# A fused attention and SwiGLU kernel on one core: other first loads, another place for two weight conversions, and DMA issue order left to the planner from the fourth pair on

## The chip, the cores and the metric

One core of one Trainium2 chip runs the whole kernel in one launch. The metric is the device time of the execution in microseconds. TensorE's granted clock is shown by the profile as a share of full speed; its two levels are 1.2 and 2.4 GHz.

## The reference

Attention over 4 batches of 8 heads, 576 positions and head size 64, with rotary embedding; its output, transposed to 2304 tokens by 512, goes through a SwiGLU block with 1536 hidden columns. All arrays are float32.

```
rotate(x) = [x1*cos - x2*sin, x1*sin + x2*cos]          # x1, x2: halves of the head
s   = rotate(q) @ rotate(k)^T / sqrt(64)
p   = exp(s - max(s)) ; p = p / (sum(p) + 1e-9)
x   = (p @ v) as 2304 x 512
out = (silu(x @ w_gate) * (x @ w_val)) @ w_out
```

## The kernel before

**Pairs and steps.** The 32 heads are worked as 16 pairs of heads. A pair has nine blocks of query rows, so there are 144 steps, n = 9p + b. Step n issues the score matmuls of block n+1 (`scores`, line 348), their row maximum on VectorE (`peak`, 363), the exponential on ScalarE (`exp`, 381), the transposes of the exponentials of block n-1 (`trans`, 424), with their high and low parts (425, 426), and some of the matmuls with V (`pv_some`, 464). All products are made from a high part and a low part of each operand.

**What a pair needs first.** `load_qk` (170) brings Q and K of a pair into one of two buffers X. `rope` (209 to 211), on GpSimd, rotates them with the tables `tab`. `qk_T` transposes the result on TensorE, and its high and low parts go to the tile N (307, 311). `qk_stack` (318 to 325) is eight DMAs of N, within SBUF, into QK, QZ and BD, from which most scores are computed; blocks 0 to 5, 9 and 10 read N directly. `load_v` (187) brings V into the one buffer VR, and `vsplit` (277, 278), on GpSimd, makes its two parts in VS.

**Start.** `start()` does the first pair by hand: VectorE rotates K (`turn(ve, 0, 1, ...)`) and the first rows of Q, GpSimd the rest. `warm` issues matmuls whose result nobody reads. ScalarE scales the table for Q (238). The table comes in three pieces on ScalarE's DMA queue, the first X in four on SyncE's.

**Two weight conversions within the attention.** `wfirst(0, i)` loads a block of the gate weights (i = 0) or value weights (i = 1) into the one buffer R (752) and returns nine operations (`bits10`: ScalarE takes the absolute value at 734, GpSimd clamps at 709, VectorE does bit work at 736 to 739, ScalarE copies at 710, GpSimd ends at 712 and 713). `PLAN["cv"]` holds for each i the step of the load and then the steps of the nine operations. Two more such conversions, `conv1`, begin in pair 15.

**Later pairs.** From pair 4 on, `xload` and `xprep` bring attention results back from DRAM (Xab, 625) and GpSimd prepares them as input of the second part (632 to 635); `rload` (618) brings the reciprocals into the same buffer R.

**What sets the order.** Each engine, and each engine's DMA queue, executes its instructions in order. In a block under `manual_schedule(engines)` the order on those engines is the order of the program text; on the others a planner orders instructions at build time by its own estimate of when each is ready. In the loop over the steps GpSimd is by hand throughout, TensorE in the first nine steps, and SyncE, which issues nearly all DMAs, in all 144 steps (`ctl0`). ScalarE and VectorE are the planner's, but an operation of a conversion stays behind what was issued before it on its engine.

Of the kernel before, what the change touches and what calls it, by code (L numbers as in the profile page):

```python
# [10 lines left out]
FP32 = mybir.dt.float32  # L11
# [25 lines left out]
    lqk=0,  # L37
# [3 lines left out]
    rstore=0,  # L41
    cv=[[5, 9, 9, 12, 13, 14, 16, 16, 17, 17], [23, 25, 26, 30, 31, 32, 34, 34, 35, 35]],
    xs=[[4, 6], [5, 5], [6, 5], [7, 5], [8, 7], [9, 5], [10, 5], [11, 5], [12, 7], [13, 7], [14, 1], [14, 2],
# [7 lines left out]
def rope_tables():  # L51
    inv = 1.0 / 10000.0 ** (np.arange(0, HALF, dtype=np.float32) / HALF)
    fr = np.outer(np.arange(S, dtype=np.float32), inv)
    cos, sin = np.cos(fr), np.sin(fr)
    c = np.concatenate([cos, cos], axis=1)
    s = np.concatenate([-sin, sin], axis=1)
    tab = np.zeros((128, 2, 5, D), np.float32)
    sc = np.float32(D ** -0.5)
    for t, full in enumerate((c, s)):
        main = full[:512].reshape(128, 4, D)  # L60
        tab[:, t, 0:4] = main
        tab[:64, t, 4] = full[512:] * sc
        tab[64:, t, 4] = full[512:]
    return tab

# [31 lines left out]
def r32(ap):  # L97
    return ap.bitcast(FP32)
# [10 lines left out]
class Attn:  # L109
    def __init__(self, tc, ctx, early, scx, qk, vr, tab, yd, rd):  # L110
# [18 lines left out]
        pairbufs(one, 0)  # L129
        self.tab = one.tile([128, 2, 9, D], FP32, name="tabs")  # L130
        self.VR = one.tile([128, 10, D], FP32, name="VR")
# [33 lines left out]
    def load_qk(self, p):  # L165
        X = self.x_p.tile([128, NSLOT, D], FP32, name="X")
        self.X[p] = X
        sy, ac = self.nc.sync.dma_start, self.nc.scalar.dma_start
        if p:
            sy(out=X, in_=self.qk[p])  # L170
            return

        def cut(d, t, src, a, z):
            d(out=t[..., a:z, :], in_=src[..., a:z, :])

        def rows(a, z):
            for d, t, src, x in ((sy, X, self.qk[p], 8), (ac, self.tab, self.tab_src, None)):
                v = (lambda y: y[:, 8:16].rearrange("p (h r) d -> p h r d", r=4)[:, :, a:z]) if x else (lambda y: y[:, :, a:z])
                d(out=v(t), in_=v(src))
        cut(sy, X, self.qk[p], 16, 18)  # L180
        cut(ac, self.tab[:, :, 0:5], self.tab_src, 4, 5)
        rows(0, 2)
        rows(2, 4)
        cut(sy, X, self.qk[p], 0, 8)

# [3 lines left out]
    def turn(self, e, p, g, ra=0, rz=4, own=True):  # L189
        X, rot = self.X[p], self.rot[p]  # L190
        C, Sn = self.tab[:, 0], self.tab[:, 1]
        m = rz - ra
# [4 lines left out]
        if g < 2:  # L197
            x = X[:, 8 * g:8 * g + 8].rearrange("p (h r) d -> p h r d", r=4)[:, :, ra:rz]
            o = rot[:, 8 * g:8 * g + 8].rearrange("p (r h) d -> p h r d", h=2)[:, :, ra:rz]
            tb = lambda t, u: t[:, None, 5 - 5 * g + ra:5 - 5 * g + rz, u].to_broadcast([128, 2, m, u.stop - u.start])  # L200
            t2 = tt[:, 0:m * 2].rearrange("p (h r) d -> p h r d", r=m)
            sel = lambda t, u: t[:, :, :, u]
        else:
            x, o = X[:, 16:18], rot[:, 16:18]
            tb = lambda t, u: t[:, 4:5, u].to_broadcast([128, 2, u.stop - u.start])
            t2 = tt[:, 0:2]
            sel = lambda t, u: t[:, :, u]
# [11 lines left out]
    def start(self):  # L219
# [10 lines left out]
        def warm(n):  # L230
            for _ in range(n):
                nc.tensor.matmul(pw[:, 0:128], self.ident, self.ident, start=True, stop=True)
        w = PLAN["warm"]
        warm(w[0])
        self.turn(po, 0, 2)
        self.turn(ve, 0, 1, 0, 2, False)
        self.turn(ve, 0, 1, 2, 4, False)
        nc.scalar.mul(self.tab[:, :, 5:9], self.tab[:, :, 0:4], float(D ** -0.5))
        self.turn(ve, 0, 0, 0, 1)
# [3 lines left out]
        for o in (64, 0):  # L243
            T(pt[:, o:o + 128], rf[:, 1024:1152], self.ident)
        kt(0), kt(1)
        warm(w[1])
        kt(2), kt(3)
        warm(w[2])
# [258 lines left out]
class Moe:  # L507
# [197 lines left out]
    def bits10(self, raw, X, hi, lo):  # L705
        nc, po = self.nc, self.nc.gpsimd
        Hf, Xf = r32(raw)[:, :, 1], r32(X)
        ops = self.bits(raw, lo, po, Xf, Xf)
        return [ops[0], lambda: po.tensor_scalar(out=Xf, in0=Xf, scalar1=W_LO, scalar2=W_HI, op0=ALU.max, op1=ALU.min)] + ops[2:5] + [
            lambda: nc.scalar.copy(hi, Hf),  # L710
# [261 lines left out]
@with_exitstack  # L972
def attn_swiglu(ctx: ExitStack, tc: tile.TileContext, qk, vr, wg, wv, wo, tab, out):
    nc = tc.nc
# [9 lines left out]
    early, scx = ExitStack(), ExitStack()  # L984
    at = Attn(tc, actx, early, scx, qk, vr, tab, yd, rd)
    ve, po = nc.vector, nc.gpsimd
# [100 lines left out]
    for n in range(NB):  # L1087
# [3 lines left out]
        if (p, b) == (NP - 1, 0):  # L1091
            assert not cvq
            early.close()
            moe.open_early(mctx)
        if b == P["lqk"] and p + 3 < NP:
            at.load_qk(p + 3)
        if b == P["lv"] and p + 1 < NP:
            at.load_v(p + 1)
        for name in P["order"]:
            steps[name](n, p, b)  # L1100
    assert not pend and not xq
    ctl0.__exit__(None, None, None)
    ctl2 = tc.manual_schedule(engines={getattr(mybir.EngineType, e) for e in ("PE", "Activation", "DVE", "SP")})
# [273 lines left out]
```

## Time and profile before

| | |
|---|---|
| median of three runs | 741.4 us (740.22 to 742.09) |
| profiled execution | 742.2 us |
| its span, first to last instruction | 740.4 us |
| TensorE busy, of the span | 706.2 us, 95% |
| VectorE, GpSimd, ScalarE busy | 542.0, 473.5, 408.8 us |
| mean granted clock | 0.986 |
| DMA | 143.86 MB, mean 194 GB/s |

A row of instructions names its start, its duration, its engine and source line, the tile written and the tiles read, and in brackets how long the engine was idle before it and what ended that. SPq and ACTq are the DMA queues of SyncE and ScalarE; their duration is that of the issue, not of the transfer.

### The profile page before, as it was taken

Reading aid. Unit: us, or ns where it says so; the run is one execution under the profiler, and the core shown is the slowest. Engines: PE = TensorE matmul, PEld = TensorE weight load, DVE = VectorE, ACT = ScalarE, POOL = GpSimd, SP = SyncE. Lnnn points to the kernel's source line nnn. Section 1 sums busy time; section 2 is a strip of 40 time slices with the busy share of each in tenths; the row PEclk is TensorE's granted clock in tenths of the full one; section 3 lists DMA queues with packets and bytes.
Section 4 is the critical chain, followed back from the end, with each engine's and each line's share of the span. In section 5 each row is a group of like instructions: output and inputs, shape, how many; then the busy total and the mean of one; then the engine's idle time right before and its main releaser. Section 6 shows DMA issues by size and latency. Waiting matters only on the chain.

```text
span 740.4 us, 12808 instructions
## 1 busy us (share of the span) xinstructions
PE 706.2 (95%) x4360; PEld 664.5 (90%) x4360; DVE 542.0 (73%) x890; ACT 408.8 (55%) x888; POOL 473.5 (64%) x471
## 2 busy tenths in 40 slices
PE   7799899999999998889899999999999999999997
PEld 6699898999899997889799999999999977888887
DVE  4788787898788885585998877868676884555451
ACT  3777898888888886446554342424334333343231
POOL 6967787999799946784997655567664856300000
PEclk9999999999999999899999999999999999999999
DMA  4967669888988978686247564564637965688661
GB/s 148 222 157 204 164 177 232 215 209 207 230 206 212 211 178 218 180 243 201 87 142 212 159 194 147 164 187 146 195 108 207 329 242 191 255 277 267 207 212 29
DMA packets 112257, 143.86 MB, mean 194 GB/s; under 512 B 18096, under 2 KB 87232, under 8 KB 112192
## 3 DMA queue, kind: packets, MB, share of 16 engines
q1 hardware_dynamic: 106976, 137.64, 65.6%
q10 hardware_dynamic: 5216, 5.39, 2.2%
q8 instruction: 35, 0.57, 0.3%
q14 instruction: 30, 0.25, 0.1%
HBM read 76.35 MB, written 42.54 MB: 161 GB/s over the span
## 4 chain that ended last, share of the span: by engine, by line
PE 70%; DMA 11%; DVE 6%; ACT 6%; issue 2%; POOL 2%; SPq 2%; ACTq 0%; DVEq 0%; POOLq 0%
PE ch L823 27%; PE ch L940 12%; PE pv L464 9%; PE sc L348 8%; PE tr L424 6%; DMA QK<-N 3%; PE ch L891 3%; DMA HF<-hf 2%; PE ch L775 2%; ACT E L381 2%; PE tr L288 1%; DMA raw<-in_moe_w_gate_dram 1%; ACT N L307 1%; DMA QZ<-N 1%; POOL fl L683 1%
## 5 line engine op out<-in xcount | busy, mean ns | idle before, releaser
L363 DVE TENSOR_REDUCE nmt<-sc 128x1 f32<-128x576 f32 x144 | 108.3, 753 | 30.1 <-PE sc L348 29.1
L381 ACT ACTIVATE E<-sc,nmt 128x576 f32<-128x576 f32 x128 | 97.3, 760 | 8.7 <-DVE nmt L363 8.6
L424 PE MATMUL tr<-ident,E 128*128 128x128 f32 x512 | 78.5, 277 | 5.8 <-ACT E L381 5.5
L807 POOL TENSOR_TENSOR u<-u,z 128x384 f32<-128x384 f32 x30 | 30.5, 1017 | 71.3 <-DVE sg L807 63.6
L424 PEld LDWEIGHTS tr<-ident,E 128*128 128x128 f32 x512 | 62.4, 142 | 8.4 <-ACT E L381 5.7
L348 PE MATMUL sc<-QK 128*128 128x288 f32 x240 | 59.3, 328 | 10.0 <-DMA QK<-N 4.7
L826 ACT COPY c<-ch 128x384 f32<-128x384 f32 x30 | 14.4, 480 | 83.3 <-PE ch L823 45.1
L209 POOL TENSOR_TENSOR t<-X,tabs 128x256 f32<-128x256 f32 (+2 forms) x94 | 53.9, 596 | 8.3 <-DVE rot L211 5.9
L425 ACT CAST ET2h<-tr 128x512 fp32r<-128x512 f32 x80 | 47.0, 588 | 18.6 <-PE tr L424 18.4
L683 DVE TENSOR_TENSOR hl<-hg,hh 128x384 fp32r<-128x384 f32 x44 | 26.2, 595 | 39.3 <-ACT hh L683 39.3
L426 DVE TENSOR_TENSOR ET2l<-tr,ET2h 128x512 fp32r<-128x512 f32 x80 | 53.1, 683 | 1.5 <-ACT ET2h L425 1.5
L940 PE MATMUL ch<-Oh,hh 128*128 128x512 f32 (+1 forms) x144 | 54.0, 375 | 0.0
L940 PE MATMUL ch<-Oh,hl 128*128 128x512 f32 (+1 forms) x144 | 53.9, 374 | 0.0
L940 PE MATMUL ch<-Ol,hh 128*128 128x512 f32 (+1 forms) x144 | 53.8, 374 | 0.0
L348 PE MATMUL sc<-N,QZ 128*128 128x288 f32 x240 | 52.2, 299 | 0.0
L211 POOL TENSOR_TENSOR rot<-rot,t 128x512 f32<-128x512 f32 (+2 forms) x47 | 47.4, 1009 | 3.7
L348 PEld LDWEIGHTS sc<-QK 128*128 128x128 f32 x240 | 37.0, 191 | 14.2 <-ACT E L381 7.9
L426 DVE TENSOR_TENSOR ET1l<-tr,ET1h 128x512 fp32r<-128x512 f32 x64 | 42.9, 687 | 8.4 <-ACT ET1h L425 8.2
L210 POOL TENSOR_TENSOR rot<-X,tabs 128x512 f32<-128x512 f32 (+2 forms) x47 | 47.2, 1003 | 0.0
L807 DVE TENSOR_TENSOR sg<-ch,u 128x384 f32<-128x384 f32 x60 | 33.4, 557 | 16.2 <-PE ch L823 13.0
L425 ACT CAST ET1h<-tr 128x512 fp32r<-128x512 f32 x64 | 36.6, 597 | 15.3 <-PE tr L424 15.3
L683 ACT CAST hh<-hg 128x384 fp32r<-128x384 f32 x44 | 22.6, 514 | 40.0 <-DVE hg L927 40.0
(413 smaller groups left out, 2431.4 us busy)
## 6 DMA issues: line engine op xcount, KB each, us to landing
QK<-N SPq DMA_DIRECT2D x64, 288.0 KB, 4.6
hg<-ht SPq DMA_DIRECT2D x22, 768.0 KB, 6.5
HF<-hf SPq DMA_DIRECT2D x12, 896.0 KB, 5.2
X<-in_qk_dram SPq DMA_DIRECT2D x15, 576.0 KB, 5.4
yd<-Y SPq DMA_DIRECT2D x31, 256.0 KB, 3.6
ht<-sg SPq DMA_DIRECT2D x20, 384.0 KB, 3.5
hf<-sg SPq DMA_DIRECT2D x20, 384.0 KB, 3.4
ht<-sg SPq DMA_DIRECT2D x20, 320.0 KB, 3.0
```

What stands on the lines that cost most here:

```text
L209: e.tensor_tensor(out=sel(t2, u), in0=sel(x, w), in1=tb(Sn, u), op=ALU.mult)
L348: nc.tensor.matmul(ps[:, g, 0:288], l, rr[:, o + g * 288:o + (g + 1) * 288], start=(x == 0), stop=(x == len(terms) - 1))
L363: nc.vector.tensor_reduce(out=nmcol, in_=ps[:, :, 0:288], axis=AX.XY, op=ALU.max, negate=True)
L381: nc.scalar.activation(out=E.rearrange("p (a b) -> p a b", a=2), in_=ps[:, :, 0:288], func=ACTF.Exp, bias=nmcol, scale=1.0, accum_out=self ...
L424: nc.tensor.transpose(ps[:, c], E[:, o + c * 128:o + (c + 1) * 128], self.ident)
L425: nc.scalar.copy(dst[0], src)
L426: nc.vector.tensor_tensor(out=dst[1], in0=src, in1=r32(dst[0]), op=ALU.subtract)
L464: nc.tensor.matmul(st["ps"][:, 0:w], VS[:, sl, :], t, start=(x == 0), stop=(x == last))
L683: return [lambda: self.nc.scalar.copy(h, f), lambda: le.tensor_tensor(out=l, in0=f, in1=r32(h), op=ALU.subtract)]
L807: add = lambda e, out, in0, in1: e.tensor_tensor(out=out, in0=in0, in1=in1, op=ALU.add)
L823: nc.tensor.matmul(acc, l[:, w, c * 128:(c + 1) * 128], r, start=(n == 0), stop=(n == 5))
L940: self.nc.tensor.matmul(ps, l[:, f], r[:, z], start=(n == 0), stop=(n == 3 * NFF - 1))
```

## The change

The rotary table becomes two arrays of the input, the four main rows and the tail, each loaded in one DMA of whole runs (2 KB and 512 bytes a partition); the first X comes in three pieces, 16:18, 8:16 and 0:8, instead of four. The rotation of K on VectorE is one turn of four rows instead of two turns of two. A ScalarE copy of one column, whose result nobody reads, stands ahead of the rest. In `bits10` the clamp is made on VectorE. The two conversions move from steps 5 to 17 and 23 to 35 to steps 13 to 26 and 27 to 35. The loads of X for pair 3 and V for pair 1 come behind the stack of pair 1, at step 6, instead of at steps 0 and 4. SyncE is by hand in the first 27 steps only.

```diff
-    cv=[[5, 9, 9, 12, 13, 14, 16, 16, 17, 17], [23, 25, 26, 30, 31, 32, 34, 34, 35, 35]],
+    cv=[[13, 16, 17, 21, 22, 23, 25, 25, 26, 26], [27, 29, 30, 30, 31, 32, 34, 34, 35, 35]],
...
-        self.tab = one.tile([128, 2, 9, D], FP32, name="tabs")
+        self.tab = [one.tile([128, 2, n, D], FP32, name=f"tab{n}{x}") for x, n in enumerate((4, 4, 1))]
...
-        cut(sy, X, self.qk[p], 16, 18)
-        cut(ac, self.tab[:, :, 0:5], self.tab_src, 4, 5)
-        rows(0, 2)
-        rows(2, 4)
-        cut(sy, X, self.qk[p], 0, 8)
+        main, tail = self.tab_src
+        sy(out=X[:, 16:18], in_=self.qk[p][:, 16:18])
+        ac(out=self.tab[2], in_=tail)
+        sy(out=X[:, 8:16], in_=self.qk[p][:, 8:16])
+        ac(out=self.tab[1], in_=main)
+        sy(out=X[:, 0:8], in_=self.qk[p][:, 0:8])
...
+        nc.scalar.copy(self.et_p.tile([128, 640], FP32, name="Et")[:, 0:1], r32(self.BD[0])[:, 0, 0:1])
         warm(w[0])
         self.turn(po, 0, 2)
-        self.turn(ve, 0, 1, 0, 2, False)
-        self.turn(ve, 0, 1, 2, 4, False)
-        nc.scalar.mul(self.tab[:, :, 5:9], self.tab[:, :, 0:4], float(D ** -0.5))
+        self.turn(ve, 0, 1, 0, 4, False)
+        nc.scalar.mul(self.tab[0], self.tab[1], float(D ** -0.5))
...
-        kt(0), kt(1)
         warm(w[1])
-        kt(2), kt(3)
+        for i in range(4):
+            kt(i)
...
-        return [ops[0], lambda: po.tensor_scalar(out=Xf, in0=Xf, scalar1=W_LO, scalar2=W_HI, op0=ALU.max, op1=ALU.min)] + ops[2:5] + [
+        return ops[:5] + [
...
-        if b == P["lqk"] and p + 3 < NP:
+        if n == 27:
+            ctl0.__exit__(None, None, None)
+        if b == P["lqk"] and 0 < p < NP - 3:
             at.load_qk(p + 3)
-        if b == P["lv"] and p + 1 < NP:
+        if b == P["lv"] and 0 < p < NP - 1:
             at.load_v(p + 1)
         for name in P["order"]:
             steps[name](n, p, b)
+            if name == "qk" and n == P["qk"][0][2]:
+                at.load_v(1)
+                at.load_qk(3)
     assert not pend and not xq
-    ctl0.__exit__(None, None, None)
```

## Rows read from the trace of the kernel before

**Rows 1.** Busy time by stretch: us, PE, PEld, DVE, ACT, POOL, clock, DMA, GB/s.

```profile
30.00:40.00 10.00, 6.68 (x38) 5.93 (x38) 4.53 (x8) 4.80 (x14) 9.68 (x11) 0.83 1.00 247
70.00:80.00 10.00, 7.26 (x48) 6.76 (x47) 6.45 (x11) 6.55 (x17) 5.44 (x7) 0.86 0.54 155
...
120.00:130.00 10.00, 8.92 (x74) 8.64 (x73) 7.14 (x13) 7.63 (x21) 6.12 (x8) 1.00 0.89 224
...
290.00:300.00 10.00, 4.48 (x33) 4.28 (x33) 4.53 (x6) 2.44 (x6) 6.87 (x8) 0.79 0.96 281
```

**Rows 2.** Instructions in order of time, the start: VectorE and ScalarE.

```profile
7.65 0.49 DVE L209 TENSOR_TENSOR Et<-X,tabs 128x128 f32<-128x128 f32 x2 [0.77 <-DMA tabs<-in_rope_dram]
7.70 1.28 ACT L238 ACT_TABLE_LOAD   x1 [7.70 <-DMA tabs<-in_rope_dram]
8.06 0.42 DVE L210 TENSOR_TENSOR rot<-X,tabs 128x256 f32<-128x256 f32 x1
...
8.99 0.63 ACT L238 ACTIVATE tabs<-tabs 128x512 f32<-128x512 f32 x1
...
9.71 0.36 DVE L209 TENSOR_TENSOR t<-X,tabs 128x64 f32<-128x64 f32 x2 [0.78 <-ACT tabs L238]
...
10.31 0.29 DVE L211 TENSOR_TENSOR rot<-rot,t 128x128 f32<-128x128 f32 x1
```

**Rows 3.** DMA rate in 40 equal slices of the first 10 us.

```profile
GB/s 0 0 0 0 0 0 0 131 146 159 201 249 223 201 225 199 209 186 242 258 338 361 356 348 399 371 418 344 449 408 387 295 148 55 18 18 0 0 0 0
```

**Rows 4.** VectorE's groups by shape, first 90 us: count, busy us, mean ns.

```profile
L311 DVE TENSOR_TENSOR N<-tr,N 128x512 fp32r<-128x512 f32 x9 | 6.2, 684 | 3.7 <-ACT N L307 3.7
```

**Rows 5.** SyncE's DMA issues ahead of the second pair's scores.

```profile
23.57 0.54 SPq L170 DMA_DIRECT2D X<-in_qk_dram  x1
...
25.74 0.42 SPq L752 DMA_DIRECT2D R<-in_moe_w_gate_dram  x1
26.25 0.60 SPq L318 DMA_DIRECT2D QK<-N  x1
```

**Rows 6.** Instructions in order of time, 35 to 47 us: GpSimd and TensorE.

```profile
35.82 1.54 POOL L278 TENSOR_TENSOR VS<-VR,VS 128x640 fp32r<-128x640 f32 x1
...
36.87 0.82 PE L348 MATMUL sc<-QK 128*128 128x288 f32 x2 [3.32 <-DMA QK<-N]
...
46.84 0.36 PE L464 MATMUL pv<-ET1h,VS 128*128 128x256 f32 x1
```

**Rows 7.** SyncE's DMA issues around the fourth pair's stack.

```profile
59.24 0.60 SPq L318 DMA_DIRECT2D QK<-N  x1
...
66.33 0.62 SPq L325 DMA_DIRECT2D BD<-N  x1
...
69.04 0.53 SPq L752 DMA_DIRECT2D R<-in_moe_w_val_dram  x1
```

**Rows 8.** The page's DMA issues: count, KB, median us from issue to landing.

```profile
QK<-N SPq DMA_DIRECT2D x64, 288.0 KB, 4.6
```

**Rows 9.** Instructions in order of time, the value weights' conversion.

```profile
74.04 0.66 ACT L734 ACTIVATE R<-R 128x512 f32<-128x512 f32 x1 [2.53 <-DMA R<-in_moe_w_val_dram]
...
74.78 1.92 POOL L709 TENSOR_SCALAR R<-R 128x512 f32<-128x512 f32 x1 [4.39 <-ACT R L734]
```

**Rows 10.** Instructions in order of time, end of the attention: SyncE, GpSimd, VectorE, TensorE.

```profile
274.25 2.56 SPq L625 DMA_DIRECT2D Xab<-yd  x4
...
278.57 1.01 POOL L632 TENSOR_TENSOR Xab<-Xab 128x384 f32<-128x384 f32 x1 [10.47 <-DMA Xab<-yd]
...
284.45 1.24 SPq L618 DMA_DIRECT2D R<-rd  x2
...
288.41 0.54 SPq L752 DMA_DIRECT2D raw<-in_moe_w_gate_dram  x1
...
295.47 1.20 DVE L733 TENSOR_SCALAR raw<-raw 128x512 uint32<-128x512 uint32 x1 [6.43 <-DMA raw<-in_moe_w_gate_dram]
...
298.85 1.12 PE L424 MATMUL tr<-ident,E 128*128 128x128 f32 x4 [5.52 <-ACT E L381]
```

More of the change, by code (lines that the diff above doesn't have):

```diff
@@ L56, in rope_tables @@
     s = np.concatenate([-sin, sin], axis=1)
-    tab = np.zeros((128, 2, 5, D), np.float32)
-    sc = np.float32(D ** -0.5)
+    main = np.zeros((128, 2, 4, D), np.float32)
+    tail = np.zeros((128, 2, D), np.float32)
     for t, full in enumerate((c, s)):
[L60 to L64, printed above, removed]
+        main[:, t] = full[:512].reshape(128, 4, D)
+        tail[:64, t] = full[512:] * np.float32(D ** -0.5)
+        tail[64:, t] = full[512:]
+    return main, tail
 def pair_rows(q, k, v):
@@ L171, in load_qk @@
             return
[L173 to L179, printed above, removed]
-        cut(sy, X, self.qk[p], 16, 18)
-        cut(ac, self.tab[:, :, 0:5], self.tab_src, 4, 5)
-        rows(0, 2)
-        rows(2, 4)
-        cut(sy, X, self.qk[p], 0, 8)
+        main, tail = self.tab_src
[4 more added lines that the diff above has]
+        sy(out=X[:, 0:8], in_=self.qk[p][:, 0:8])
     def load_v(self, p):
@@ L190, in turn @@
         X, rot = self.X[p], self.rot[p]
-        C, Sn = self.tab[:, 0], self.tab[:, 1]
+        C, Sn = self.tab[g][:, 0], self.tab[g][:, 1]
         m = rz - ra
@@ L199, in turn @@
             o = rot[:, 8 * g:8 * g + 8].rearrange("p (r h) d -> p h r d", h=2)[:, :, ra:rz]
-            tb = lambda t, u: t[:, None, 5 - 5 * g + ra:5 - 5 * g + rz, u].to_broadcast([128, 2, m, u.stop - u.start])
+            tb = lambda t, u: t[:, None, ra:rz, u].to_broadcast([128, 2, m, u.stop - u.start])
             t2 = tt[:, 0:m * 2].rearrange("p (h r) d -> p h r d", r=m)
@@ L204, in turn @@
             x, o = X[:, 16:18], rot[:, 16:18]
-            tb = lambda t, u: t[:, 4:5, u].to_broadcast([128, 2, u.stop - u.start])
+            tb = lambda t, u: t[:, 0:1, u].to_broadcast([128, 2, u.stop - u.start])
             t2 = tt[:, 0:2]
@@ L972, in attn_swiglu @@
 @with_exitstack
-def attn_swiglu(ctx: ExitStack, tc: tile.TileContext, qk, vr, wg, wv, wo, tab, out):
+def attn_swiglu(ctx: ExitStack, tc: tile.TileContext, qk, vr, wg, wv, wo, main, tail, out):
     nc = tc.nc
@@ L984, in attn_swiglu @@
     early, scx = ExitStack(), ExitStack()
-    at = Attn(tc, actx, early, scx, qk, vr, tab, yd, rd)
+    at = Attn(tc, actx, early, scx, qk, vr, (main, tail), yd, rd)
     ve, po = nc.vector, nc.gpsimd
@@ L1364 @@
     host[_INS[5]] = np.ascontiguousarray(inputs[_INS[5]])
-    host["rope"] = rope_tables()
+    host["rope"], host["tail"] = rope_tables()
     for name, a in host.items():
```

## The prediction

> **What bounds the kernel now.** I read the busy time by stretches of 10 us first, then TensorE's waits in the order of time, then SyncE's queue around each of them. From 90 to 280 us TensorE is full: the stretch of 120 to 130 us is among the emptiest there, and has it busy for 8.92 us at full clock [rows 1]. So time is to be had only where it stands still. There are four such places: the start, and the other three stretches of [rows 1]. A stretch's price is 10 us less its PE busy time times its granted clock. From 30 to 40 us that is 10 - 6.68 x 0.83 = 4.5 us, from 70 to 80 us 10 - 7.26 x 0.86 = 3.8 us, from 290 to 300 us 10 - 4.48 x 0.79 = 6.5 us. In each the clock had fallen from 2.4 to 1.2 GHz for part of the stretch after TensorE had been idle, so a wait costs more than its own length. These prices are estimates, since the clock is a mean over idle time too. A smaller kind of stop is that of 120 to 130 us, 1.1 us, where a pair begins. What TensorE gains before 280 us should reach the end, since nothing ahead of it is bound to an absolute time.
>
> **The start.** Before, VectorE begins the second half of K's rotation at 7.65 us, when the last table piece has landed, and ends it at 8.93 us (the next row's 9.71 less its 0.78 of idle). ScalarE gets the same landing at 7.70 us, loads its function table for 1.28 us, scales for 0.63 us, and only then can VectorE turn the first rows of Q, done at 10.60 us [rows 2]. After the change the table load stands behind two DMA issues and a memset, some 5 us before the main table lands, and costs nothing. What is late next is VectorE itself: K comes in one turn. Its two products of 128x256 cost 0.42 each [rows 2] and the two operations of 128x512 0.68 each [rows 4], 2.2 us with gaps; twice the half turn, 2 x 1.28 = 2.6 us, is the upper bound, and the scaling (0.63 us) hides beside it. With the turn of Q, 0.36 + 0.28 + 0.29, the end is L + 3.2 us if the main table lands at L, against 10.60: the gain is 7.4 - L. So hiding the table load gains nothing unless the table lands earlier.
>
> When does it land? The pieces of short runs move at 131 to 258 GB/s until about 5 us, and the long runs behind them at 338 to 449 GB/s [rows 3]. One DMA instead of two saves one issue as well. 640 KB lie in the tails, K and the main table together; at 350 GB/s they would be moved in 1.9 us from the first byte at 1.75 us, but the next loads share the engines. I take L = 5.8 us, a gain of 1.6 us. The bounds are L = 7.65 (a loss of 0.2) and L = 5.0 (a gain of 2.4).
>
> The Trainium skill (DMA: Bandwidth & Descriptors, Specifications) has runs of 512 bytes and more at line rate. The old table and K pieces were 512-byte runs, so by it their length gains nothing, L would be about 7.0 and the gain 0.4 us, the sum 1.2 us less. This trace speaks against it: the rate rose from 258 to 338 GB/s and more only when the 2 KB runs came up, though a start-up of the queues could look the same. The skill also (ScalarE: Activation LUTs, What ACT_TABLE_LOAD costs) puts a drain of 1.38 us on top of the load's 1.28. Here the ACTIVATE begins 0.01 us after the load's end, so no such drain is seen; with it the old start would have had 1.4 us more to give.
>
> **The second pair's stack.** Before, SyncE issues three loads (X, V and gate weights, first and last shown), 1.4 MB by their shapes, between 23.57 and 26.2 us, and the eight stack DMAs behind them [rows 5]. At the 247 GB/s of that stretch 1.4 MB take 5.7 us. The score matmuls wait 3.32 us for QK [rows 6]. After the change none of the three is ahead. With the start 1.6 us earlier the stack begins at 24.7. A stack without loads ahead of it takes 7.7 us of issue, 59.24 to 66.95 [rows 7], and a QK copy lands 4.6 us after its issue [rows 8]. The three DMAs that the first waiting block needs are issued by 24.7 + 2.2 (estimated from the same stack), so landed at 31.5; it is wanted at 36.87 - 3.32 - 1.6 = 31.95. The next block may wait some tenths. I take 4.0 of the 4.5 us; between 2 and 4.5.
>
> What is late next: V of pair 1 is issued behind the stack, at about 32.5, and lands some 4.6 us later (the QK copy, of about its size [rows 8]). GpSimd's second part takes 1.54 us, both some 2.3 by that (an estimate), so VS is ready at 39.5, against 37.36 before; its first reader, at 46.84 before [rows 6], comes at about 41.2. That cover is 1.7 us. X of pair 3 lands at about 39, when GpSimd is through with V; the clamp that stood there before (1.92 us) is gone. No cost taken; up to 1.5 us if the cover goes.
>
> **The conversions.** Before, the value weights are issued at 69.04 us, behind the stack and V [rows 7]; ScalarE, in order, stands at their absolute value until 74.04 us for 2.53 us with the next exponential behind it [rows 9], and TensorE starves: the 3.8 us. That wait goes. But the new plan has two places like it. The gate weights' load comes at step 13, right behind the stack of step 12 and V: the old value weights, in such a place, landed 74.04 - 59.24 = 14.8 us after the stack's start [rows 7, 9] (two stores stood between, which may not now). Its first operation is at step 16, four steps behind the stack, and a step is about 2.2 us: the stacks at 26.25 and 59.24 us [rows 5, 7] lie 13 steps apart, 33 us less the 4.5 us stop. Whether ScalarE waits depends on how far back the planner puts that operation. The value weights' load at step 27 needs the buffer R, which GpSimd gives back with its last operation of step 26, and has its first operation at step 29, two steps later as before. Both may wait at the old price (a loss of 3.8) or neither (a gain of 3.8). I take half of the old price once: a gain of 1.9 us. The clamps leave GpSimd (2 x 1.92 us [rows 9], which waits 4.39 us there anyway) and come to VectorE at about 0.68 each, nearest row of that size [rows 4]; between 0 and 1.4 us, taken as 0, because TensorE is what is full there.
>
> **SyncE by the planner.** From step 27 a DMA no longer stands behind another that waits for a buffer. The clearest case is the end of the attention. SyncE issues two Xab loads only at 274.25 us, behind the last stack; GpSimd, idle for them for 10.47 us until 278.57, gives back R late, SyncE stands before R<-rd until 284.45, and behind that the raw weights are issued at 288.41. VectorE, in order, waits 6.43 us for them with the row maxima behind it, ScalarE for these, TensorE 5.52 us [rows 10]. If one Xab load goes ahead of the stack, or raw ahead of R<-rd, this shrinks. The other side: loads put ahead of a stack make the stack late, as at 120 to 130 us, 1.1 us a pair [rows 1], and 11 or 12 stacks are the planner's. I take half of the 6.5 us and give back 0.7 for pair starts: 2.5 us. The bounds are a gain of 7.8 (the whole stop and the low clock behind it) and a loss of 13.
>
> **Sum.** 1.6 + 4.0 + 1.9 + 2.5 = 10.0 us from the profiled execution's 742.2 (span 740.4 and 1.8 around it) gives 732.2. That execution lies 0.8 above the median of the runs, so on their scale I forecast 731.5 us.
>
> **Rivals.** (1) All waits go: 1.6 + 4.5 + 3.8 + 7.8 = 17.7, so 724 us. For it: each has its cause in SyncE's order or place. Against: the planner's estimate put the old waiting operations where they waited too. (2) The waits move: ScalarE stands for both conversions (2 x 3.8 instead of 3.8), and the end of the attention stays as it is; 742.2 - 1.6 - 4.0 + 3.8 is 740.4, on the runs' scale 739.6, no change. For it: some 14 us of landing against four steps, 9 us. (3) Slower, by one mechanism: the planner issues loads of X, V and Xab ahead of the stack as soon as their buffer is free, and TensorE waits at each pair's start. 1.1 us at 11 pairs are 12.1, and without a gain at the attention's end 742.2 - 7.5 + 12.1 = 746.8, 746 on the runs' scale. It decides from seven pairs on, where the 7.5 us of the other terms are used up. For it: 7.7 + 4.6 = 12.3 us from the stack's start to its last landing, where its first use comes eight steps, about 17 us, after it. Against: most stacks come long after their buffers are free. (4) The whole runs don't land sooner: the start gives nothing, 733 us, within the forecast's own range.
>
> **Chances.** Forecast (726 to 738) 0.48, rival 1 0.20, rival 2 0.12, rival 3 0.17, others slower 0.03. Less than 0.3% (2.2 us) can't be told from no change. Faster takes the first two and a little of rival 2: 0.70. Same 0.10. Slower 0.20. The range for 8 in 10, with the unknown SyncE term, is 721 to 745; the forecast's own is 726 to 738.
>
> **What would show it.** Right: the function table load before 4 us and K's rotation in one go at about 5.8; no wait for QK between 30 and 40 us; granted clock 1.0 there; ScalarE's absolute values without idle before them; Xab issued before the last stack and VectorE's wait at raw shortened. Wrong: the main table lands after 7 us; ScalarE idle before line 734 twice; TensorE waits for QK or QZ at most pair starts after step 27; the attention's end as late as before.

## The result and the profile after

The changed kernel takes 729.12 us (median of four runs, 727.35 to 730.19), against 741.0 us for the kernel before in the same runs: ratio 0.9836 [0.9812, 0.9861]. The forecast was 731.5 us. The profiled execution takes 730.19 us with a span of 728.4 us, 12.0 us less than before. The time is right, but two of the forecast's four terms are not: the conversions cost time where they were to give some, and SyncE's order gave nearly four times its term.

Busy time by stretch of the kernel after (us, PE, PEld, DVE, ACT, POOL, clock, DMA, GB/s), against [rows 1]:

```profile
30.00:40.00 10.00, 9.82 (x78) 9.42 (x76) 8.14 (x13) 8.49 (x22) 7.17 (x10) 1.00 0.79 230
50.00:60.00 10.00, 6.04 (x34) 5.50 (x35) 4.64 (x8) 5.60 (x13) 9.60 (x13) 0.83 0.81 228
70.00:80.00 10.00, 8.37 (x65) 7.97 (x65) 8.02 (x14) 7.12 (x17) 9.60 (x12) 1.00 0.61 178
...
120.00:130.00 10.00, 9.89 (x81) 9.49 (x80) 8.94 (x16) 9.22 (x25) 9.51 (x13) 1.00 0.72 195
290.00:300.00 10.00, 9.58 (x62) 9.21 (x61) 4.94 (x7) 4.56 (x11) 6.13 (x6) 1.00 0.53 150
```

The stops at 30 to 40 and at 290 to 300 us are gone, clock 1.00 in both. A new one stands at 50 to 60 us, worth 10 - 6.04 x 0.83 = 5.0 us by the prediction's measure. The pair starts of 120 to 130 us got better, not worse.

To see where time is won and lost I take the start of the n-th block's exponential on ScalarE (144 of them, in order of time, the first is block 0) in the kernel before, less the same start in another kernel: its lead at block n. Changes of the lead from one block to the next show where the gain lies. These leads, from one execution each, with the medians of all runs beside them (us; ratios are to the kernel before in the same runs):

```
                             lead at block                                median  ratio
kernel                       0     9    11    22    35   135   140   142
after                     2.07  2.08  6.53  2.04  2.76  3.97  3.96 11.06  729.12  0.9836 [0.9812, 0.9861]
SyncE by hand throughout  2.00  2.00  6.44 -0.05  2.13  2.14  2.13  2.04  739.36  0.9967 [0.9942, 0.9991]
SyncE by hand to step 117 2.07 -1.62  2.81 -3.32 -1.16 -0.78 -3.18  3.05  734.10  0.9905 [0.9875, 0.9935]
conversions later         1.56  1.35  5.79  6.78  7.89  8.93  4.27 10.51  728.72  0.9841 [0.9806, 0.9876]
old load order            1.10  1.13  5.56  0.50  2.62  4.75  4.74 11.52  730.07  0.9845 [0.9810, 0.9880]
old conversions           1.72  1.72  5.89  5.47  6.11  7.64  7.62 14.33  725.57  0.9795 [0.9761, 0.9829]
both old                  0.81  0.93  5.06  4.36  4.19  5.69  5.68 11.89  730.39  0.9851 [0.9822, 0.9880]
old start                 1.20  1.22  5.65 -0.54  1.64  3.21  3.20  9.67  732.21  0.9876 [0.9845, 0.9907]
old clamp                 0.82  0.94  5.38  0.24  3.29  6.06  0.17  6.41  731.27  0.9878 [0.9838, 0.9917]
later, end steps put off  1.03  1.27  5.71  6.71  7.79  8.18  8.18 14.83  730.37  0.9836 [0.9803, 0.9870]
later, raw by ScalarE     2.25  2.04  6.48  7.49  8.55 10.02 11.29 16.21  724.68  0.9777 [0.9747, 0.9807]
gate old, value later     2.00  2.02  6.18  5.67  8.50  8.23  3.80 10.03  730.83  0.9860 [0.9829, 0.9891]
the same, raw by ScalarE  1.40  1.62  5.78  4.84  8.39  8.77 10.03 15.66  726.24  0.9793 [0.9765, 0.9822]
```

In the kernel after, the lead is made of 2.1 us at the start, 4.5 at blocks 9 to 11, 1.8 more by block 18, a loss of 6.3 by block 22, 1.9 more by 135, and 7.1 at blocks 140 to 142. The start, in order of time (VectorE and ScalarE), against [rows 2]:

```profile
1.66 1.28 ACT L227 ACT_TABLE_LOAD   x1 [1.66 <-PEq L1357]
5.29 0.76 DVE L202 TENSOR_TENSOR Et<-X,tab 128x256 f32<-128x256 f32 x2 [3.89 <-DMA tab<-in_rope_dram]
5.29 0.63 ACT L231 ACTIVATE tab<-tab 128x512 f32<-128x512 f32 x1 [2.14 <-DMA tab<-in_rope_dram]
...
7.88 0.29 DVE L204 TENSOR_TENSOR rot<-rot,t 128x128 f32<-128x128 f32 x1
```

The function table is loaded 2.3 us before it is needed, K turns in one go from 5.29 us, and the first rows of Q are done at 8.17 us, not 10.60. The DMA rate of the first 10 us, against [rows 3]:

```profile
GB/s 0 0 0 0 0 0 0 86 209 344 238 164 221 238 221 279 393 320 311 418 416 397 408 432 367 461 406 369 442 184 19 0 0 0 0 0 0 0 0 0
```

The rate stays above 300 GB/s from 4.0 us on, not from 5.0. SyncE's queue around the second pair's stack, against [rows 5]:

```profile
23.59 0.59 SPq L311 DMA_DIRECT2D QK<-N  x1
...
31.42 0.54 SPq L180 DMA_DIRECT2D VR<-in_vr_dram  x1
```

The stack starts where the loads stood. The conversions, against [rows 7, 9], in order of time (SyncE, ScalarE, TensorE):

```profile
47.52 0.52 SPq L745 DMA_DIRECT2D R<-in_moe_w_gate_dram  x1
53.05 0.66 ACT L727 ACTIVATE R<-R 128x512 f32<-128x512 f32 x1 [4.10 <-DMA R<-in_moe_w_gate_dram]
54.24 0.46 PE L457 MATMUL pv<-ET2h,VS 128*128 128x320 f32 x1 [3.69 <-ACT ET2h L418]
...
80.20 0.67 ACT L727 ACTIVATE R<-R 128x512 f32<-128x512 f32 x1 [1.65 <-DMA R<-in_moe_w_val_dram]
```

ScalarE, in order, stands 4.10 us for the gate weights; the high parts of the transposes (L418) are behind it, and TensorE waits 3.69 us for these. That is the stop at 50 to 60 us. The value weights have the same wait, shorter; in the five other kernels with these steps it is 0 to 0.28 us, while the gate weights' is 4.14 to 5.24 in all of them. The end of the attention, against [rows 10] (SyncE, GpSimd, VectorE):

```profile
261.73 1.27 SPq L618 DMA_DIRECT2D Xab<-yd  x2
263.09 0.61 SPq L311 DMA_DIRECT2D QK<-N  x1
...
265.99 1.02 POOL L625 TENSOR_TENSOR Xab<-Xab 128x384 f32<-128x384 f32 x1 [4.39 <-DMA Xab<-yd]
269.49 1.23 SPq L611 DMA_DIRECT2D R<-rd  x2
273.47 0.54 SPq L745 DMA_DIRECT2D raw<-in_moe_w_gate_dram  x1
281.83 0.71 DVE L726 TENSOR_SCALAR raw<-raw 128x512 uint32<-128x512 uint32 x1
```

The two Xab loads that stood behind the last stack at 274.25 us now go ahead of its QK copies, at 252.84 and (shown) 261.73 us. GpSimd waits 4.39 us, for the second of them, instead of 10.47 for the first, R comes at 269.49 instead of 284.45, the raw weights are asked for 15 us earlier, and VectorE meets them without idle time.

### The profile page after: what moved, and what is told of

It reads as the page before. It is cut to its first block, busy times and chain, and to the rows that moved or that the text cites. A ratio compares the mean times of both kernels' runs of the same rounds, so it can differ in the third digit from the quotient of the medians.

```text
span 728.4 us, 12775 instructions
## 1 busy us (share of the span) xinstructions
PE 702.2 (96%) x4360; PEld 659.8 (91%) x4360; DVE 542.7 (75%) x888; ACT 408.7 (56%) x889; POOL 468.1 (64%) x469
## 4 chain that ended last, share of the span: by engine, by line
PE 67%; DMA 11%; DVE 7%; ACT 6%; POOL 3%; issue 3%; SPq 2%; ACTq 0%; POOLq 0%; DVEq 0%
PE ch L816 28%; PE ch L933 13%; PE pv L457 8%; PE sc L341 7%; PE tr L417 6%; PE ch L884 3%; DMA HF<-hf 2%; DMA QK<-N 2%; ACT E L374 2%; DMA raw<-in_moe_w_gate_dram 2%; DMA raw<-in_moe_w_val_dram 1%; DMA ht<-sv 1%; PE tr L281 1%; ACT N L300 1%; PE pv L225 1%
## 5 line engine op out<-in xcount | busy, mean ns | idle before, releaser
L202 POOL TENSOR_TENSOR t<-X,tab 128x256 f32<-128x256 f32 (+2 forms) x94 | 53.7, 593 | 5.9 <-DVE rot L204 3.4
L418 ACT CAST ET2h<-tr 128x512 fp32r<-128x512 f32 x80 | 47.0, 588 | 16.4 <-PE tr L417 16.0
L203 POOL TENSOR_TENSOR rot<-X,tab 128x512 f32<-128x512 f32 (+2 forms) x47 | 47.0, 1001 | 0.0
L800 DVE TENSOR_TENSOR sg<-ch,u 128x384 f32<-128x384 f32 x60 | 33.4, 557 | 16.3 <-PE ch L816 13.3
L418 ACT CAST ET1h<-tr 128x512 fp32r<-128x512 f32 x64 | 36.6, 596 | 14.7 <-PE tr L417 14.5
L457 PE MATMUL pv<-ET2h,VS 128*128 128x320 f32 x128 | 41.1, 331 | 3.9 <-ACT ET2h L418 3.7
```

The source lines that it names most:

```text
L202: e.tensor_tensor(out=sel(t2, u), in0=sel(x, w), in1=tb(Sn, u), op=ALU.mult)
L418: nc.scalar.copy(dst[0], src)
L457: nc.tensor.matmul(st["ps"][:, 0:w], VS[:, sl, :], t, start=(x == 0), stop=(x == last))
L800: add = lambda e, out, in0, in1: e.tensor_tensor(out=out, in0=in0, in1=in1, op=ALU.add)
```

## The experiments

A difference of two ratios times 741 us is what separates two kernels that did not run together. Such a difference has an interval of some 3 us either way.

**SyncE by hand throughout.**

```diff
-        if n == 27:
-            ctl0.__exit__(None, None, None)
...
     assert not pend and not xq
+    ctl0.__exit__(None, None, None)
```

> The changed kernel with SyncE by hand to the end of the loop, everything else as changed. Theory A (the stop at the attention's end went because the planner issues the Xab, R and raw loads ahead of what they stood behind): the stop of 5 to 6 us near 290 us comes back with VectorE waiting 5 us or more at the raw weights, and two or more pair starts lose about 1 us again; 736 to 738 us. Rival B (the stop went because the attention ends earlier or the conversions moved, SyncE's order is neutral): 728 to 730 us and no stop there.

739.36 us, (0.9967 - 0.9836) x 741 = 9.7 us slower than after, and somewhat above Theory A's range. In order of time, SyncE, VectorE and TensorE at the attention's end:

```profile
282.10 1.24 SPq L611 DMA_DIRECT2D R<-rd  x2
286.07 0.54 SPq L745 DMA_DIRECT2D raw<-in_moe_w_gate_dram  x1
...
293.48 1.15 DVE L726 TENSOR_SCALAR raw<-raw 128x512 uint32<-128x512 uint32 x1 [6.57 <-DMA raw<-in_moe_w_gate_dram]
...
296.82 1.11 PE L417 MATMUL tr<-ident,E 128*128 128x128 f32 x4 [5.80 <-ACT E L374]
```

This is the old stop with its old chain, as Theory A has it. Its lead at block 135 is 1.8 us less than after's, and the 7.1 us of the end are missing whole. So the planner's order is worth nearly ten microseconds, most of it at this one place.

**SyncE by hand to step 117.**

```diff
-        if n == 27:
+        if n == 117:
```

> The changed kernel with SyncE by hand until step 117 (pair 13) instead of step 27. Theory A1 (only the last three pairs need the planner): the stop at the attention's end stays away, a pair start or two loses 1 us, 729 to 732 us. Rival A2 (the gain needs loads moved ahead over many pairs): part of the stop comes back, 733 to 737 us.

734.10 us, 5.1 us slower than after by the ratios, whose intervals lie apart: Rival A2's time. From block 135 to 142 the lead rises by 3.8 us here, against 7.1 in after and -0.1 by hand throughout. So the order in the last three pairs gives about half of the 9.7 us, and does not suffice. The leads of this one execution are moreover low by 3.7 us from block 9 on for a reason outside the edit. Its stretches of 10 to 30 us (columns as above):

```profile
10.00:20.00 10.00, 9.34 (x55) 7.46 (x55) 5.50 (x9) 5.16 (x12) 9.53 (x13) 0.83 0.70 167
20.00:30.00 10.00, 10.00 (x55) 9.38 (x56) 6.82 (x11) 6.52 (x16) 9.61 (x13) 0.66 0.31 67
```

TensorE is as busy as in the kernel after at 10 to 20 us (9.31) but runs partly at 1.2 GHz, where after shows 1.00; TensorE's instructions stand in the same order in both. That is not what makes the median slower: the other five executions have mean clocks of 0.990 to 0.992, like after's 0.990 to 0.995, and take 731.60 to 737.07 us. Where the order between steps 27 and 117 gives the other half was not followed.

**Conversions later.**

```diff
-    cv=[[13, 16, 17, 21, ...], [27, 29, 30, 30, 31, 32, 34, 34, 35, 35]],
+    cv=[[13, 20, 20, 21, ...], [27, 32, 32, 33, 33, 34, 34, 34, 35, 35]],
```

> The changed kernel with the first operations of both conversions later: gate weights' absolute value and clamp at step 20 instead of 16 and 17, value weights' at step 32 instead of 29 and 30. Theory C (ScalarE's waits for the two loads, 4.1 and 1.7 us, cost TensorE about 6 us with the low clock): both waits go, the lead over the kernel before stays at 7 us or more at step 39 instead of 2.1, 723 to 725 us. Rival D (the lead is lost to another wait, such as the next late transfer or the shorter room for the last operations): 728 to 730 us.

728.72 us, the same as after, as in Rival D. ScalarE's wait for the gate weights is gone (6.78 us of lead at block 22, not 2.04; the one for the value weights stays, 1.91 us), and 8.93 us stand at block 135. But 4.7 of these are lost by block 140. In order of time, GpSimd, SyncE, VectorE:

```profile
261.81 2.91 SPq L618 DMA_DIRECT2D Xab<-yd  x4
268.40 1.02 POOL L625 TENSOR_TENSOR Xab<-Xab 128x384 f32<-128x384 f32 x1 [8.77 <-DMA Xab<-yd]
...
270.53 1.25 SPq L611 DMA_DIRECT2D R<-rd  x2
...
273.55 0.54 SPq L745 DMA_DIRECT2D raw<-in_moe_w_gate_dram  x1
...
281.25 1.26 DVE L726 TENSOR_SCALAR raw<-raw 128x512 uint32<-128x512 uint32 x1 [4.29 <-DMA raw<-in_moe_w_gate_dram]
```

Attention is 5 us further, yet the raw weights are asked for at 273.55 us, as in the kernel after (273.47): they stand behind R on SyncE's queue, R waits until GpSimd has given back the only buffer R, and GpSimd waited 8.77 us for Xab. The Xab load that GpSimd waits for is issued when it is in after (261.81 and 261.73 us), but here that is behind the last stack (its first QK copy is issued at 257.46), there ahead of it (263.09); GpSimd has its data at 268.40 us instead of 265.99. The prediction's chain of [rows 10] is back in short form, and it eats what was won ahead of it.

**Old load order** (third X and second V ahead of the second pair's stack).

```diff
-        if b == P["lqk"] and 0 < p < NP - 3:
+        if b == P["lqk"] and p + 3 < NP:
...
-        if b == P["lv"] and 0 < p < NP - 1:
+        if b == P["lv"] and p + 1 < NP:
...
-            if name == "qk" and n == P["qk"][0][2]:
-                at.load_v(1)
-                at.load_qk(3)
```

> The changed kernel with the loads of X for pair 3 and V for pair 1 back at steps 0 and 4, ahead of the second pair's stack. Theory E (the 4.5 us won at the stack carry to the end): TensorE waits for QK again at about 33 us and the time is 733 to 734 us. Rival F (the 4.5 us are given back at once where ScalarE waits for the gate weights, since that wait ends at a landing): the wait at the weights shrinks by about as much and the time is 729 to 730 us.

730.07 us, not told apart from after. Its lead still rises by 4.4 us at blocks 9 to 11: the stop at 30 to 40 us does not come back. Both theories had it come back, so Rival F's time (729 to 730) came without its reason.

**Old conversions.**

```diff
-    cv=[[13, 16, 17, 21, ...], [27, 29, 30, 30, 31, 32, ...]],
+    cv=[[5, 9, 9, 12, 13, 14, 16, 16, 17, 17], [23, 25, 26, 30, 31, 32, 34, 34, 35, 35]],
```

> The changed kernel with the conversion's old places (gate weights' load at step 5, value weights' at 23, as in the kernel before), all else changed. Theory A: the wait for the second pair's stack went because the gate weights' load left step 5, not because the loads of pair 3 and of V were put behind the stack; then TensorE stands again for QK at 30 to 40 us, by 3 to 5 us, ScalarE's wait for the gate weights near 53 us (4.1 us in the changed kernel) is gone, and the lead over the kernel before is about 2 us at block 11 (6.5 in the changed kernel) and 1.5 to 3 at block 135 (4.0). Rival B, that the stack's new place did it: no wait for QK, lead 6 us at block 11, and more than the changed kernel's 4.0 at block 135, as the gate weights no longer come late: 8 us. For the end: if the gain at the attention's end (7.1 us in the changed kernel) adds to what is there before, A gives 731 to 732 us and B 725; if the end is pinned by something that does not move with the blocks, 729 to 730 under both.

725.57 us, 3.0 us faster than after by the ratios (their intervals overlap); the leads have it 3.7 us ahead at block 135. SyncE and ScalarE, and the stretch with after's stop:

```profile
3.09 0.43 SPq L745 DMA_DIRECT2D R<-in_moe_w_gate_dram  x1
...
32.38 0.68 ACT L727 ACTIVATE R<-R 128x512 f32<-128x512 f32 x1
...
69.20 0.66 ACT L727 ACTIVATE R<-R 128x512 f32<-128x512 f32 x1 [3.15 <-DMA R<-in_moe_w_val_dram]
```

```profile
50.00:60.00 10.00, 9.24 (x71) 8.99 (x72) 8.89 (x15) 9.62 (x24) 9.60 (x12) 1.00 0.79 196
```

ScalarE has no wait for the gate weights at their old steps, and the old wait for the value weights. By the leads the move of the conversions made the kernel slower; the times lean the same way. And the wait for QK is still away, with 5.89 us of lead at block 11, as Rival B has it. But this run says little of Theory A: with X and V behind the stack nothing holds up the gate weights' load, which is issued at 3.09 us, not at 25.74 [rows 5], and has landed at 10.04 us, long before the stack.

**Both old.** The two edits above together.

> The changed kernel with both undone that stand ahead of the second pair's stack on SyncE's queue: conversions' steps as before (gate weights' load at step 5) and the loads of the third X and of V at their old places ahead of the stack. Each undone alone left TensorE no wait for QK (lead over the kernel before at block 11: 5.6 and 5.9 us, against 6.5). Theory A: one of the two is enough, and together they are the old queue; TensorE stands for QK 3 to 5 us at 30 to 40 us, the lead at block 11 is 1 to 2.5 us, and the time is that of the old conversions alone (725.6) plus 3.5 to 4.5: 729 to 730 us. Rival B: the wait went for another reason (the start's earlier end): no wait, lead 5.5 to 6.5 at block 11, 725 to 726 us.

730.39 us, as Theory A gave it, but by another way: the wait for QK at 30 to 40 us has still not come back (lead up by 4.1 us at blocks 9 to 11). In order of time, GpSimd, SyncE, TensorE:

```profile
21.81 1.56 POOL L271 TENSOR_TENSOR VS<-VR,VS 128x640 fp32r<-128x640 f32 x1
22.84 0.53 SPq L169 DMA_DIRECT2D X<-in_qk_dram  x1
23.47 0.38 SPq L180 DMA_DIRECT2D VR<-in_vr_dram  x1
23.90 0.42 SPq L745 DMA_DIRECT2D R<-in_moe_w_gate_dram  x1
24.85 0.60 SPq L311 DMA_DIRECT2D QK<-N  x1
...
32.79 0.51 PE L341 MATMUL sc<-QK 128*128 128x288 f32 x2 [0.17 <-DMA QK<-N]
```

The same three loads stand ahead of the stack as in [rows 5], and TensorE waits 0.17 us. X is issued 0.7 us earlier than before, but the gate weights 1.8 us earlier. In the kernel before, SyncE stood between the two; its waits of 22 to 30 us there (us in total, times, longest):

```profile
SPq L187 <- POOL VS L278: 1.2, 1, 1.2
```

V's buffer came back late because GpSimd's work, unbroken from 10.83 us before and from 8.87 us here, was 2 us later at V's second part. So V and the gate weights are issued 1.9 and 1.8 us earlier and the stack 1.4: V lands at 27.67 us instead of 30.83, and TensorE has its QK at 32.79 instead of 36.87. The loads were not through when the stack came: the first QK copy is issued at 24.85, V lands 2.8 us after that. Why the landings gain more than the issues is open (from 26 to 28 us 371 GB/s are moved here, 239 before). All this is read from the two traces and was not tried alone. The 4.1 us (by the ratios) between this kernel and the one with old conversions alone are in part a start 0.9 us later and 1.0 more by block 35; the rest lies mostly behind the attention and was not followed.

**Old start.** The rotary table, first loads, first turns and start() of the kernel before; the core of it:

```diff
-        nc.scalar.copy(self.et_p.tile([128, 640], FP32, name="Et")[:, 0:1], r32(self.BD[0])[:, 0, 0:1])
...
-        self.turn(ve, 0, 1, 0, 4, False)
-        nc.scalar.mul(self.tab[0], self.tab[1], float(D ** -0.5))
+        self.turn(ve, 0, 1, 0, 2, False)
+        self.turn(ve, 0, 1, 2, 4, False)
+        nc.scalar.mul(self.tab[:, :, 5:9], self.tab[:, :, 0:4], float(D ** -0.5))
```

> The changed kernel with the whole start of the kernel before: one table of five parts cut in pieces, first loads in pieces, no copy ahead of ScalarE's table load, first rotations as before. Theory A: the start is worth what block 0's lead shows, 2.1 us, and it is carried to the end: 731.2 us, lead 0 at block 0, 2 us less than the changed kernel's at every later block. Rival B: a later stop takes it (the lead at block 9 or at the attention's end is that of the changed kernel): 729 us, unchanged.

732.21 us, 3.0 us slower than after by the ratios, whose intervals overlap. ScalarE:

```profile
6.49 1.28 ACT L238 ACT_TABLE_LOAD   x1 [6.49 <-DMA tabs<-in_rope_dram]
...
55.07 0.66 ACT L734 ACTIVATE R<-R 128x512 f32<-128x512 f32 x1 [5.24 <-DMA R<-in_moe_w_gate_dram]
```

The same start put the main table down at 6.49 us here and at 7.70 in the kernel before, and this kernel has a lead of 1.20 us at block 0 though its start is the old one. Across the twelve profiled executions with the new start the table lands at 5.00 to 6.27 us and the lead at block 0 is 0.81 to 2.25. The mean of these twelve is 1.56 us, that of the two old starts (0 and 1.20) 0.60: the start is worth about 1 us at block 0 by that, and one execution can't size it. The gate weights then land later too (5.24 us of ScalarE's idle, not 4.10).

**Old clamp** (the conversion's clamp on GpSimd).

```diff
-        return ops[:5] + [
+        return [ops[0], lambda: po.tensor_scalar(out=Xf, in0=Xf, scalar1=W_LO, scalar2=W_HI, op0=ALU.max, op1=ALU.min)] + ops[2:5] + [
```

> The changed kernel with the conversion's clamp back on GpSimd instead of VectorE (two operations in all). Theory A, as in the prediction: nothing, 728 to 730 us, ratio to the kernel before 0.981 to 0.987, lead at block 135 within 0.7 us of the changed kernel's 4.0. Rival B: GpSimd is late for V's split behind it and TensorE waits 1 to 2 us: 730 to 732 us. Rival C: VectorE is what the blocks wait for at the conversions, and the clamp back on GpSimd gives 1 us: 727.5 to 728.5 us.

731.27 us; 3.1 us slower by the ratios, whose intervals overlap, so unclear. The time is Rival B's, but no loss shows at the conversions. The profile has it ahead of after at block 135 (6.06 against 3.97) and then losing 5.9 us at the end. SyncE and VectorE:

```profile
261.01 0.61 SPq L311 DMA_DIRECT2D QK<-N  x1
...
265.17 2.13 SPq L618 DMA_DIRECT2D Xab<-yd  x2
...
274.37 1.23 SPq L611 DMA_DIRECT2D R<-rd  x2
278.04 0.41 SPq L745 DMA_DIRECT2D raw<-in_moe_w_gate_dram  x1
...
285.77 0.83 DVE L726 TENSOR_SCALAR raw<-raw 128x512 uint32<-128x512 uint32 x1 [5.95 <-DMA raw<-in_moe_w_gate_dram]
```

Again R behind GpSimd and raw behind R, now later than in any other kernel with the planner's order from step 27. The trace shows another order on SyncE's queue: the second of the two Xab loads is issued behind the last stack, where after has it ahead. All kernels with the planner's order from step 27 fall in two by this. In after, old load order, old conversions, both old and old start that load is ahead of the last stack, and the lead is the same at blocks 135 and 140 within 0.02 us. In conversions later, old clamp and gate old, value later it is behind, and 4.4 to 5.9 us are lost there. The remaining three have it behind too, and an edit at the raw weights. What moves the load, GpSimd's two longer operations or something else, was not tried.

**Later conversions, end steps put off.** The steps on the raw weights of the last pair come two blocks later.

```diff
-    c1=[[3, 3, 4, 4, 5, 5, 6, 6, 6], [7]],
+    c1=[[5, 5, 5, 6, 6, 6, 7, 7, 7], [8]],
...
-            if p == NP - 1 and b == 7 * i:
+            if p == NP - 1 and b == 8 * i:
```

> The changed kernel with the conversions' steps late, and the steps on the raw weights of the attention's end two blocks later (the first at step 5 of the last pair instead of 3, the last at 7, the next load at 8 instead of 7). Theory D: what pins the attention's end is VectorE standing in its order at the raw weights, with TensorE's row maxima queued behind; two blocks are 4 us, so most of the 4.3 us wait goes: lead 14 to 15 at block 142, time 724 to 726 us. Rival E: something else holds the blocks there, or what is put off is wanted right behind the attention: 728 to 730 us, with the lead gone again by 310 us.

730.37 us. The stop goes as Theory D has it (14.83 at block 142), and Rival E's second half comes true. SyncE, VectorE, ScalarE, TensorE:

```profile
298.01 0.35 SPq L745 DMA_DIRECT2D raw<-in_moe_w_val_dram  x1
302.68 0.69 DVE L726 TENSOR_SCALAR aux<-raw 128x512 uint32<-128x512 uint32 x1 [12.60 <-DMA raw<-in_moe_w_val_dram]
305.67 0.65 ACT L713 CAST w1h<-raw 128x512 fp32r<-128x512 f32 x1 [10.04 <-DVE raw L730]
308.21 0.69 PE L768 MATMUL ch<-xm1h,w0h 128*128 128x384 f32 x1 [6.80 <-ACT Xab L783]
```

The value weights use the same buffer, so they come later by as much; ScalarE stands at their high part with the evictions behind it, and TensorE waits 6.80 us.

**Later conversions, raw weights on ScalarE's queue.** With the late steps of above:

```diff
-        self.nc.sync.dma_start(out=tmp[:, 0:1024], in_=self.wsrc(i, f))
+        (self.nc.scalar if (f, i) == (1, 0) else self.nc.sync).dma_start(out=tmp[:, 0:1024], in_=self.wsrc(i, f))
```

> The changed kernel with the conversions' steps late (its own run gave 728.7 us: 8.9 us ahead of the kernel before at block 135, but only 10.5 at block 142) and the load of the first raw weights of the attention's end issued on ScalarE's queue at its place in the order, no longer on SyncE's, where it stood behind the load of R, which waited 5.2 us for GpSimd. Theory D: VectorE's wait of 4.3 us for the raw weights goes, as they are asked for some 4 us earlier; lead 14 to 16 at block 142, time 723.5 to 726 us. Rival E: the transfer itself is slow there or waits for freed memory (it took 7.7 us from issue to landing), so VectorE stands as long: 728 to 729 us. Rival F: ScalarE stands at the issue for the freed buffer: 729 to 732 us.

724.68 us, ratio 0.9777 [0.9747, 0.9807], below the whole interval of after, so faster than both kernels and 4.7 us faster than with the late steps alone. In order of time, ScalarE's queue, SyncE's, VectorE:

```profile
268.45 0.35 ACTq L745 DMA_DIRECT2D raw<-in_moe_w_gate_dram  x1
268.86 1.25 SPq L611 DMA_DIRECT2D R<-rd  x2
...
276.62 0.42 DVE L726 TENSOR_SCALAR raw<-raw 128x512 uint32<-128x512 uint32 x1
```

Asked for 5.1 us earlier, the weights are there in time, and the lead goes up at the end instead of down. The place on the queue was the cause, as Theory D has it.

**Gate at its old steps, value late.**

```diff
-    cv=[[13, 16, 17, 21, ...], [27, 29, 30, 30, 31, ...]],
+    cv=[[5, 9, 9, 12, 13, 14, 16, 16, 17, 17], [27, 32, 32, 33, 33, 34, 34, 34, 35, 35]],
```

> The changed kernel with the gate weights' conversion at its old steps and the value weights' at the late ones (load at step 27, first operation at 32). Theory A: both of ScalarE's waits are gone, the gate's near 53 us and the value's near 70 to 80 us, and nothing is lost at either: lead 8 to 9.5 us at block 35 and at block 135 (old conversions alone: 6.1 and 7.6), TensorE free of the wait for the gate weights as there. At the attention's end the raw weights are then asked for no earlier than before (273.5 us in the run with late conversions), so VectorE stands 2 to 4 us: lead 12 to 14 at block 142, 725 to 727 us. Rival B: the blocks' lead is carried through the end: 723 to 724 us.

730.83 us, above the range of both theories. The leads at blocks 35 and 135 (8.50 and 8.23) are as Theory A has them, the loss at the end is larger (10.03 at block 142, not 12 to 14):

```profile
281.77 1.22 DVE L726 TENSOR_SCALAR raw<-raw 128x512 uint32<-128x512 uint32 x1 [4.12 <-DMA raw<-in_moe_w_gate_dram]
```

**The same, raw weights on ScalarE's queue.** The edit of two experiments above on this kernel.

> The last run's kernel, and the load of the first raw weights of the attention's end on ScalarE's queue. Theory A: the lead of 8 to 9.5 us at block 135 is carried and the stop of the kernel before at the attention's end falls away too: lead 15 to 17 at block 142, 722 to 724.5 us, the fastest of all. Rival B: as in the run with late conversions and this load, 1 to 2.5 us of it are lost again behind the attention (TensorE for an eviction, VectorE 7 us for the next raw weights): 724 to 726 us.

726.24 us, 4.6 us faster than without that edit, and with a ratio of 0.9793 against 0.9777 no better than with the gate late too. The lead at block 142 (15.66) is Theory A's, the time is next to Rival B's. But nothing is lost behind the attention, as Rival B had it: the lead is 15.09 us at block 143 and 16.3 at the end of the span. That gain of 1.2 us is small beside the 3.9 us of the kernel with old conversions.

## Why the prediction was right

The sum was 10.0 us and the profiled execution is 12.0 us faster. That it comes so close is in part luck: by the runs the conversions came out 4.9 us below their term and SyncE's order 7.2 us above, and these two errors cancel for the most part.

- **Start, 1.6 us.** Right in its mechanism: the table load is out of the way, K turns in one go, 5.29 + 3.2 = 8.5 us for the end that came at 8.17. The lead says 2.07 us here and 0.81 to 2.25 in twelve executions; the old start alone varies by 1.2, and put back it costs 3.0 us with overlapping intervals. So the size, about 1 to 3 us, agrees but is not settled. That short runs were what made it late is not borne out: in the kernel after some 500 KB move up to 4.0 us (the rates times a quarter of a microsecond), mostly at 164 to 279 GB/s, though only the 128 KB of the tails are short runs; from 2.5 us on the trace's packets are of 2 KB, but for 6 KB. That looks like the start-up that the prediction left as the other reading. The Trainium skill (DMA: Bandwidth & Descriptors, Specifications), by which the 512-byte runs were at line rate already, fits in so far as their length was not what held them; the landing at about 7.0 us worked out from it does not, as the latest of twelve was 6.27. Rival 4's premise is out: all twelve landings are earlier than both with the old start (6.49 and 7.70).
- **Second pair's stack, 4.0 us.** The size is right (4.5 us of lead at blocks 9 to 11), its reason is not the only one. Neither the loads' new order, nor the conversion's new step, nor the start is needed alone: each was undone and the gain stayed, and it stayed when order and step were undone together. Three loads ahead of the stack cost TensorE 0.17 us when the last is issued 1.8 us earlier. The failing step is that the stop was priced as the loads' size over a rate (1.4 MB at 247 GB/s, 5.7 us) and put down to their place alone. What it hung on in its stead, as far as the traces show, is when they are issued, and so when SyncE got V's buffer back; that was not tried alone.
- **Conversions, +1.9 us.** Wrong in sign: -3.0 us by the runs (intervals overlap), -3.7 by the leads at block 135. The prediction named the mechanism and its two places, and took half of one price; both waits came (4.10 and 1.65 us of ScalarE), as in rival 2 and in its own sign of being wrong, and the lead falls by 6.3 us at the first. The old value wait was given up for a new gate wait where there had been none. What failed is the step from "four steps behind the stack" to "may or may not wait": the 14.8 us of landing that it had read, against some 9 us of steps, spoke for the wait. The landing came 15.0 us after the stack's start (38.01 to 53.03), and ScalarE stood there from 48.95 us, 10.9 us after it.
- **SyncE by the planner, 2.5 us.** Too small: 9.7 us. The whole stop at the attention's end went, 7.1 us, where half of 6.5 was taken, by the prediction's own chain and with the earlier sign that it named (Xab ahead of the last stack). Nothing was lost at pair starts: the lead rises by 1.2 us from block 35 to 135, and by hand throughout it does not change; rival 3 needed the opposite. But that the planner puts Xab ahead is no rule: in other kernels of this case it does not, and part of the stop is back. With the order by hand to step 117 about half of the 9.7 us is gone.
- **Clamps, 0.** Unclear: put back, the kernel is slower by 3.1 us with overlapping intervals, and the trace shows this at the raw weights, behind another place of an Xab load, not at the clamp.

Undone one at a time, the parts take 3.0 (start), 0.7 (load order), -3.0 (conversions), 9.7 (planner) and 3.1 us (clamp), 13.5 in all against 12.2 for the change; each difference has an interval of some 3 us either way, so the sum agrees, but only the planner's part stands well clear of the noise.

Rival 1's time, 724 us for the case that all waits go, was reached by the kernel with late conversions and the raw weights off SyncE's queue: 724.68 us.

Left open: the lead's change behind block 143. It is +1.5 us in the kernel after (12.06 of span less 10.56 at block 143), +4.4 with the old load order, +3.9 with old conversions and -3.5 in the kernel with the end put off; only that last one was traced to its cause.

## What to carry over

A wait on an in-order queue is paid by everything behind it, so a load is best put where its data are wanted late and what stands ahead of it on the queue waits for nobody; when it can't be, another queue is worth more than another step. Price a moved load by its landing, measured at a like place, against the steps that are left, and believe that number when it says wait. And undo parts together, not only one by one: the new start was enough to remove one stop, and so were the new order and the new step without it, so that undoing any one of the three shows nothing. An order left to the planner can change with any edit: look for the load that matters in each kernel's queue before an edit elsewhere gets the blame.

## What was not expected of the hardware

- TensorE ran at a mean granted clock of 0.83 and 0.66 from 10 to 30 us of one execution and at 1.00 in the same stretches of the kernel after, whose code is the same there and whose TensorE is as busy (9.34 against 9.31 us at 10 to 20 us). It cost 3.7 us of lead.
- The same first loads land up to 1.3 us apart from one execution to another (5.00 to 6.27 us in twelve). Three of the twelve also load the gate weights, from 3.07 to 3.09 us on; they land at 5.00, 5.42 and 5.90, among the others.
- 1.4 MB of loads ahead of the stack cost TensorE 3.32 us [rows 6] when the last of them was issued at 25.74 us [rows 5], and 0.17 us when it was issued at 23.90. Why 1.8 us make so much of a difference is open.
